# Seven experts' second product in seven block products instead of eight, rows added by accumulating DMAs, and a list schedule for the expert stage

## The chip, the cores and the metric

The kernel runs on one core of one Trainium2 chip. The metric is device time in microseconds (us) of one execution, as a median over runs. The profile was taken from one further execution. Engines are named PE (matrix products), PEld (PE's weight loads), DVE, ACT, POOL (element-wise engines) and SP, which here only issues transfers (DMAs).

## The reference

Attention for 4 batches of 8 heads (576 tokens, width 64) gives x, 2304 rows of 512. A gate gives each row a weight for each of 8 experts (softmax, then 8 rounds of normalising rows and columns). The output is the weighted sum of all experts over all rows:

```python
logits = x @ w_gate
P = np.exp(logits - logits.max())
for _ in range(8):
    P /= P.sum(1, keepdims=True) + 1e-09
    P /= P.sum(0, keepdims=True) + 1e-09
    P *= N / E
for e in range(E):                    # 8 experts: 512 -> 1024 -> 512
    h = np.maximum(x @ w1[e], 0.0)
    out += P[:, e:e + 1] * (h @ w2[e])
```

## The kernel before

Everything is float32 in and out. Matrix products run in float16: each operand is split into a high half and a low half (the remainder), and each product is the sum of three partial products, high by high, high by low and low by high. The splits are element-wise work: ACT writes the high half ("h" in names such as `w1h`), DVE or POOL writes the low half.

The program has two stages. The first holds attention, expert 0 and the gate; a list scheduler (`class Plan`) sets the order of its instructions. It gets each step with an assumed duration (`US`), a due time, its inputs and the buffers that it takes, and writes one fixed order for each engine. At its end the prepared block sums of x are stored (`x_sums`) and the weights of the first half expert are split.

The second stage holds experts 1 to 7. Each expert is cut into two halves of 512 hidden columns, which makes 14 **half experts** (`PH`). For each of these the rows are walked in five blocks (`BLK`): the rows form two halves of 1152, and a block takes 256 rows from each half, the last block 128 ("half block"). So a half expert is 4 full blocks and one half block, 4.5 blocks in all. A block has two products.

- First product, W1 by x: written as a product of 2 by 2 blocks that needs seven block products instead of eight (Winograd's form). These are `M1` to `M7` (`mm1`); each is 12 matmuls of w columns (w is 256, or 128 in a half block), whose left operands are blocks of W1 or sums of blocks (A11, A12, A22, S1 to S4) and whose right operands are blocks of x or sums of them, loaded again for each block (`ts`). The results land in four PSUM banks a to d, and DVE, ACT and POOL add them up: `m1`, `u2`, `u3`, `c12`, `c21` and `c22`. Then ACT and DVE write the relu of the four blocks as high and low halves into a tile `h` (`relu_hi`, `relu_lo`).
- Second product, h by W2 (`mm2`, steps `T0` to `T3`): for each of 4 tiles of 128 rows (2 in a half block) 12 matmuls of 512 columns. DVE multiplies the PSUM tile by the gate weight and adds it to the output accumulator in SBUF, `accA` or `accB` (`out_add`, L1165).

The order in the second stage is a table written by hand, `BLOCK_AT` with a `PERIOD` of 19.6: all steps of all blocks sorted by their place. The next half expert's weights are loaded and prepared meanwhile by a generator, `w_prep`, one step at fixed intervals (`SIDE_EVERY`). It takes the maximum of each weight tile (`absmax` on DVE, then across the partitions with POOL's `partition_all_reduce`, L221), scales to a power of two, splits seven blocks of W1 (low halves at L253) with four block sums on POOL in between (L1078 to L1089), and then four pieces of W2 without sums. The last lines of the sorting:

```python
    for n in sorted(range(len(plan)), key=lambda n: (plan[n][0], n)):
        plan[n][1]()
```

## Time and profile before

| what | value |
|---|---|
| median of 3 runs | 1782.56 us (1782.41 to 1786.26) |
| the profiled execution, its own time | 1782.06 us |
| its span, first to last instruction | 1780.2 us |
| PE busy | 1734.9 us, 97% of the span |
| DVE, ACT, POOL busy | 1107.1, 661.2, 506.9 us |

The span is what the rows below divide up; some 1.9 us of the execution's own time lie around it. Busy time is an average over both stages. PE's records overlap, since matmuls are pipelined, so that the time of one matmul is read from a run of many, not from its own duration.

### The profile page before, as it was taken

How to read it: one execution, taken by the hardware profiler on the slowest of the kernel's cores; microseconds unless marked ns; L12 is line 12 of the kernel's file. 1: busy time of each engine (PE TensorE's matmuls, PEld its weight loads, DVE VectorE, ACT ScalarE, POOL GpSimd, SP SyncE). 2: the span in 40 equal slices, each digit the busy share in tenths (PEclk: the TensorE clock that was granted, in tenths of full speed). 3: DMA queues.
4: the chain of work that ended last, by engine and by line, in shares of the span. 5: the costliest groups of instructions: out<-in, count | busy, mean ns of one | idle time of the engine just before them, and what ended most of it. 6: DMA issues, size and time to landing. Idle time of an engine off the chain costs nothing.

```text
span 1780.2 us, 32960 instructions
## 1 busy us (share of the span) xinstructions
PE 1734.9 (97%) x13860; PEld 1085.4 (61%) x13860; DVE 1107.1 (62%) x1849; ACT 661.2 (37%) x1157; POOL 506.9 (28%) x435
## 2 busy tenths in 40 slices
PE   5989999999999999999999999999999999999999
PEld 3455455554456566666666666666666666666665
DVE  7978757641895565656565656565756574656543
ACT  3568777775334332323222222222323232222221
POOL 3467788875332010201010202020202020202000
PEclk8999999999999999999999999999999999999999
DMA  5323122101023122222221222131313131213122
GB/s 203 114 93 98 42 66 95 42 17 39 24 95 115 54 82 81 74 83 88 68 90 66 88 67 106 49 107 48 107 48 107 48 107 52 103 48 107 51 89 87
DMA packets 47645, 140.18 MB, mean 79 GB/s; under 512 B 12436, under 2 KB 16904, under 8 KB 43400
## 3 DMA queue, kind: packets, MB, share of 16 engines
q1 hardware_dynamic: 47496, 138.08, 23.4%
q8 instruction: 108, 1.77, 0.4%
q14 instruction: 41, 0.34, 0.1%
HBM read 128.41 MB, written 9.64 MB: 78 GB/s over the span
## 4 chain that ended last, share of the span: by engine, by line
PE 86%; DVE 6%; DMA 3%; ACT 2%; issue 2%; POOL 1%; SPq 0%; POOLq 0%; ACTq 0%; DVEq 0%
PE m L1157 34%; PE m L1141 30%; PE g L718 5%; PE g L697 5%; PE s L415 3%; PE t L471 3%; PE av L507 3%; PE t L468 2%; DMA wraw<-in_w 1%; DVE mraw L416 1%; PE as L521 1%; DVE w1l L253 1%; DVE h L1182 1%; DMA s<-sd 1%; PE av L501 0%
## 5 line engine op out<-in xcount | busy, mean ns | idle before, releaser
L1157 PE MATMUL m<-w2h,h 128*128 128x512 f16 x2016 | 641.6, 380 | 0.0
L1157 PEld LDWEIGHTS <-h 128*128 128x128 f16 x3024 | 294.0, 98 | 303.4 <-issue 2.1
L1141 PEld LDWEIGHTS <-w1h 128*128 128x128 f16 x3920 | 369.4, 98 | 97.2 <-issue 7.0
L1157 PE MATMUL m<-w2l,h 128*128 128x512 f16 x1008 | 382.6, 380 | 0.0
L1141 PE MATMUL m<-ts,w1h 128*128 128x256 f16 (+1 forms) x2240 | 349.0, 262 | 1.0 <-DVE u L1173 1.0
L1173 POOL TENSOR_TENSOR c<-u,t 128x512 f32<-128x512 f32 (+1 forms) x70 | 81.8, 1169 | 826.2 <-DVE u L1173 734.2
L1178 ACT ACTIVATE h<-c 128x512 f16<-128x512 f32 (+1 forms) x210 | 117.3, 583 | 464.4 <-DVE c L1173 429.1
L1141 PE MATMUL m<-ts,w1l 128*128 128x256 f16 (+1 forms) x1120 | 284.6, 262 | 0.0
L1141 PE MATMUL m<-xx,w1h 128*128 128x256 f16 (+1 forms) x1680 | 261.9, 262 | 5.1 <-ACT m L1170 5.1
L1141 PE MATMUL m<-xx,w1l 128*128 128x256 f16 (+1 forms) x840 | 213.6, 262 | 0.0
L1182 DVE SCALAR_TENSOR_TENSOR h<-c,h 128x512 f16<-128x512 f32 (+1 forms) x210 | 144.4, 710 | 101.9 <-ACT h L1178 101.5
L1141 PEld LDWEIGHTS <-w1l 128*128 128x128 f16 x1960 | 191.7, 98 | 17.8
L1165 DVE SCALAR_TENSOR_TENSOR accA<-m,pp,accA 128x512 f32<-128x512 f32 x168 | 125.4, 746 | 76.6 <-PE m L1157 76.3
L486 POOL TENSOR_TENSOR eb<-e,eb 128x576 f16<-128x576 f32 x117 | 158.8, 1371 | 37.1 <-ACT eb L483 32.8
L416 DVE TENSOR_REDUCE mraw<-s 128x2 f32<-128x576 f32 x140 | 105.3, 752 | 63.9 <-PE s L415 62.7
L1165 DVE SCALAR_TENSOR_TENSOR accB<-m,pp,accB 128x512 f32<-128x512 f32 x84 | 63.0, 750 | 111.8 <-PE m L1157 111.8
L1170 ACT COPY t<-m 128x512 f32<-128x512 f32 (+1 forms) x70 | 37.9, 541 | 206.8 <-PE m L1141 206.8
L1173 DVE TENSOR_TENSOR c<-m,u 128x512 f32<-128x512 f32 (+1 forms) x140 | 88.8, 634 | 39.4 <-PE m L1141 39.4
L479 ACT ACTIVATE e<-t,ebias,pc 128x576 f32<-128x576 f32 x117 | 97.3, 832 | 34.2 <-PE t L471 30.1
L342 POOL TENSOR_TENSOR raw<-raw,trig 128x576 f32<-128x576 f32 x61 | 92.4, 1528 | 36.5 <-DMA raw<-in_qk 19.0
L415 PE MATMUL s<-Z 64*128 64x288 f16 (+1 forms) x936 | 83.5, 289 | 15.7 <-DVE mraw L416 7.3
L257 ACT ACTIVATE w1h<-wraw,s 128x512 f16<-128x512 f32 x98 | 66.9, 715 | 65.7 <-DVE s L246 54.9
(160 smaller groups left out, 2086.8 us busy)
## 6 DMA issues: line engine op xcount, KB each, us to landing
ts<-xd SPq DMA_DIRECT2D x110, 512.0 KB
wraw<-in_w SPq DMA_DIRECT2D x28, 1024.0 KB
raw<-in_qk SPq DMA_DIRECT2D x32, 576.0 KB
ts<-xd SPq DMA_DIRECT2D x28, 256.0 KB
vraw<-in_v SPq DMA_DIRECT2D x4, 1280.0 KB
rs<-si SPq DMA_DIRECT2D x64, 72.0 KB
wraw<-in_w SPq DMA_DIRECT2D x8, 512.0 KB
xd<-ts SPq DMA_DIRECT2D x8, 512.0 KB
```

The source lines that it names most:

```text
L342: engine[e].tensor_tensor(r[:, t, :], r[:, t, :], trig[:, n, :], op=ALU.mult)
L415: pe.matmul(po[j], zz[r, x, qc], zz[r, y, QH[kh]], start=n_ == 0, stop=n_ == 2)
L416: return lambda: dve.reduce_max(o, ps[:, :, 0:HS], axis=AX.X)
L479: act.activation(e32, ps[:, :, 0:HS], AF.Exp, bias=ebias, scale=sc[p][0])
L486: engine[e].tensor_tensor(E[g][:, 1], e32, E[g][:, 0], op=ALU.subtract)
L697: pe.matmul(pv, a[:, hf, c, fh, j * P : (j + 1) * P], x[:, c, :, n0 : n0 + w], start=c == 0 and n == 0, stop=c == KC - 1 and n == 2,)
L1141: pe.matmul(live[bk][:, f * w : (f + 1) * w], x[:, a, i, fs], y[:, i], start=first and f == 0 and n == 0, stop=n == 5, skip_group_check=True,)
L1157: pe.matmul(po, x, y[:, ch], start=n == 0, stop=n == 11)
L1165: dve.scalar_tensor_tensor(o, pt.pop((th, j)), pp[e, hf][:, tt : tt + 1], o, op0=ALU.mult, op1=ALU.add)
L1173: engine[e_].tensor_tensor(temp(n, tag), live[x], live[y], **add)
L1178: act.activation(t[:, 0 : 2 * w], live[src], AF.Relu)
L1182: dve.scalar_tensor_tensor(f(hq[n][:, 1]), live[src], 0.0, f(hq[n][:, 0]), op0=ALU.max, op1=ALU.subtract)
```

## The change

Second product. The second product of experts 1 to 7 takes Winograd's form too. Its left operands are the four blocks A11, A12, A21 and A22 of h and four sums S1 to S4 of them (A21 is needed only inside the sums), its right operands three blocks of W2 and four sums T1 to T4. The seven block products `N1` to `N7` (table `G2_MM`) are 12 matmuls of 256 columns each, into four PSUM banks of their own (`ps_n`; `ps_m` holds four for the first product). A half block has 6 matmuls in each.

Element-wise work. In a block, DVE now computes u2, u3, c22, c12, c21, the sums S1 to S4, five low halves (A11, A12, S2, S3, S4), and U2, U3, C22, C21, C12 of the second product: 19 operations. POOL writes two low halves (A22 and S1, `LOC`). ACT makes m1, the relus, the seven high halves and n1, and scales the four result blocks by the gate weight into a tile `ev` (`out`; 8 instructions of 256 columns). In the last half expert DVE adds the result into the accumulator itself, as before.

Adding of rows. An `ev` tile is added to the accumulator by a DMA that POOL issues with `accum_op=ALU.add` (`deliver`, two a block, 512 KB each); there are three `ev` buffers.

Weights. W2 is split in seven pieces with four block sums, as W1 is. The maximum across partitions is taken on DVE: a transpose of 32 by 32 blocks, six small maxima and two small copies (`turn`), in place of POOL's all-reduce.

Order. The list scheduler also orders the second stage (`experts`), with due times worked out from block lengths and the offsets `SH2`, `LAG`, `WSH`; the hand-written table and the side generator go. `H_BUFS`, the number of h tiles (seven are used in a block now, four before), goes from 10 to 9.

```diff
-H_BUFS = 10
+H_BUFS = 9
+LAG = 2.1
+WSH = 10.0
+SH2 = dict(m1=0.7, o21=3.7, u2=-1.5, o12=-1.5, S2=1.5, S1l=0.7, A11l=-3, A12h=0.7, o11=3.7, c21=-1.5, N1=-3, c12=0.7, C21=1.5, N5=1.5, N7=0.7, S1h=1.5)
...
+LOC = dict(A22="pool", A11="dve", A12="dve", S1="pool", S2="dve", S3="dve", S4="dve")
...
-PERIOD = 19.6
-BLOCK_AT = dict(
-    begin=-0.1, middle=0.5, ld0=6.6, ld1=15.7, M1=0.0, M6=1.3, M5=5.2, M2=6.5, M7=10.4, M3=11.7, M4=15.6,
...
-    def gmax(mx, n, tag):
-        g = small.tile([P, n], F32, tag=tag + "g", name="g")
-        pool.partition_all_reduce(g, mx, P, RMAX)
...
-        r, s, hl = yield from start(w2, 2, 4)
-        for i in range(5):
-            if i < 4:
-                hi(hl, s, i, r[:, i * 512 : (i + 1) * 512], False)
-            if i:
-                lo(hl, s, i - 1, r[:, (i - 1) * 512 : i * 512], False)
...
+        def turn(d=d):
+            t = small.tile([P, 32], F32, tag="wt", name="wt")
+            dve.transpose(t, d["g"].to_broadcast([P, 32]))
+            y = small.tile([P, 4], F32, tag="wy", name="wy")
+            for b in range(4):
+                dve.reduce_max(y[0:32, b : b + 1], t[32 * b : 32 * b + 32], axis=AX.X)
+            g = small.tile([P, 1], F32, tag="wg2", name="wg2")
+            dve.reduce_max(g[0:32], y[0:32], axis=AX.X)
+            dve.tensor_copy(g[32:64], g[0:32])
+            dve.tensor_copy(g[64:P], g[0:64])
+            d["g2"] = g
...
+        def split(i, a, deps=()):
+            put(f"wh{i}", "act", US["wh"], lambda: hi(i, a), ["ws"] + list(deps), uses=[raw])
+            put(f"wl{i}", "dve", US["wl"], lambda: lo(i, a), [f"wh{i}"], uses=[raw], lock=True)
+
+        def total(k, o, x, y, op, deps):
+            put(k, "pool", US["ptt"], lambda: pool.tensor_tensor(quad(o), quad(x), quad(y), op=op), deps, uses=[raw])
...
+            split(B11, "11")
+            split(B22, "22")
+            split(B21, "21")
+            total("w+1", "11", "12", "11", ALU.subtract, [f"wl{B11}", "wm1"])
+            total("w+3", "12", "12", "22", ALU.subtract, ["w+1"])
+            total("w+2", "22", "22", "11", ALU.subtract, ["w+3", f"wl{B22}"])
+            total("w+4", "21", "21", "22", ALU.subtract, ["w+2", f"wl{B21}"])
+            split(T1, "11", ["w+1"])
+            split(T2, "22", ["w+2"])
+            split(T3, "12", ["w+3"])
+            split(T4, "21", ["w+4"])
...
+        def mm(bank, first, lhs, rhs, step, width, pl):
+            if first:
+                live[bank] = pl.tile([P, 512], F32, tag="g", name="m")[:, 0:cols]
+            (ah, al), (bh, bl) = lhs, rhs
+            for f_ in range(cols // width):
+                n = 0
+                for i in range(2):
+                    for x, y in ((ah, bh), (ah, bl), (al, bh)):
+                        pe.matmul(
+                            live[bank][:, f_ * width : (f_ + 1) * width], step(x, i, f_), y[:, i],
+                            start=first and f_ == 0 and n == 0, stop=n == 5, skip_group_check=True,
+                        )
+                        n += 1
...
-        def mm2(th, j):
-            if j >= nt:
...
-                h = hq[("c11", "c12", "c21", "c22")[2 * (ch // 2) + th]]
-                hh, hl = h[:, 0, ch % 2, js], h[:, 1, ch % 2, js]
-                for x, y in ((hh, wh), (hh, wl), (hl, wh)):
-                    pe.matmul(po, x, y[:, ch], start=n == 0, stop=n == 11)
-                    n += 1
...
-        def out_add(th, j):
-            if j >= nt:
-                return
-            tt = th * NT2 + k * (WB // P) + j
-            o = accs(tt)
-            dve.scalar_tensor_tensor(o, pt.pop((th, j)), pp[e, hf][:, tt : tt + 1], o, op0=ALU.mult, op1=ALU.add)
...
+        def mm2(bk, first, a, b):
+            lhs = [hq[a][:, n] for n in range(2)]
+            rhs = [x[:, b].rearrange("p (c f) -> p c f", c=2) for x in ws[q][2]]
+            mm("n" + bk, first, lhs, rhs, lambda x, i, f_: x[:, i, f_ * P : (f_ + 1) * P], 256, ps_n)
...
+        def op_lo(eng, n, src):
+            h, l = (hq[n][:, i].rearrange("p c w -> p (c w)") for i in range(2))
+            engine[eng].tensor_tensor(l, live[src], h, **sub)
+
+        def plus_lo(n, src):
+            h, l = (hq[n][:, i].rearrange("p c w -> p (c w)") for i in range(2))
+            dve.scalar_tensor_tensor(l, live[src], 0.0, h, op0=ALU.max, op1=ALU.subtract)
+
+        def plus_combine(n, x, y, op1):
+            dve.scalar_tensor_tensor(live[n], live[x], 0.0, live[y], op0=ALU.max, op1=op1)
...
+        def out(th, dh, src):
+            for j in range(nt):
+                tt = th * NT2 + k * (WB // P) + j
+                x, s = live[src][:, j * 256 : (j + 1) * 256], pp[e, hf][:, tt : tt + 1]
+                d = slice(dh * 256, dh * 256 + 256)
+                if final:
+                    o = accs(tt)[:, d]
+                    dve.scalar_tensor_tensor(o, x, s, o, op0=ALU.mult, op1=ALU.add)
+                else:
+                    if th not in ev:
+                        ev[th] = evp.tile([P, 2, DM], F32, tag="ev", bufs=3, name="ev")
+                    act.activation(ev[th][:, j, d], x, AF.Copy, scale=s)
+
+        def deliver(th):
+            t0_ = k * (WB // P)
+            if final:
+                for j in range(nt):
+                    store(th * NT2 + t0_ + j)
+            else:
+                a = accparts[0][:, th, t0_ : t0_ + nt] if t0_ < ACC_A else accparts[1][:, th, t0_ - ACC_A : t0_ - ACC_A + nt]
+                pool.dma_start(out=a, in_=ev[th][:, 0:nt], accum_op=ALU.add)
...
+        put("A22h", "act", rl, tm(3) + 1.3, lambda: op_hi("A22", "c22", AF.Copy), ["r22"], [("h", "A22")], [("c22", 0)])
+        put(
+            "A22l", LOC["A22"], on[LOC["A22"]], tm(3) + 1.9, lambda: op_lo(LOC["A22"], "A22", "c22"), ["A22h"], [],
+            [("h", "A22"), ("c22", 0)], lock=True)
...
+        put("c12", "dve", pa, tm(5), lambda: plus("c12", "c", "u2"), ["M3", "u2"], [("c12", 0)], [("m", "c"), ("u2", 0)])
+        put(
+            "S1", "dve", on["dve"], tm(5) + 0.7, lambda: plus_combine("c22", "c12", "c22", ALU.add), ["c12", "A22l"], [],
+            [("c12", 0), ("c22", 0)], lock=True)
+        put(
+            "S3", "dve", on["dve"], tm(5) + 2.0, lambda: plus_combine("c12", "c12", "r11", ALU.subtract), ["S1", "r11"], [],
+            [("c12", 0), ("r11", 0)], lock=True)
+        put(
+            "S2", "dve", on["dve"], tm(5) + 1.4, lambda: combine("dve", "r11", "c22", "r11", sub), ["S3", "A11l"], [],
+            [("c22", 0), ("r11", 0)], lock=True)
...
+    G2_MM = dict(
+        N1=("a", True, B11, "A11"), N6=("b", True, T2, "S2"), N5=("c", True, T1, "S1"), N2=("a", False, B21, "A12"),
+        N7=("d", True, T3, "S3"), N3=("c", False, B22, "S4"), N4=("d", False, T4, "A22"),
+    )
...
+    def experts():
+        plan = Plan(dict(
+            m=4, n=4, m1=1, u2=1, u3=1, c22=1, r11=1, c12=1, c21=1, n1=1, U2=1, U3=1, C21=1, ev=3, h=H_BUFS, ts=3, stg=1,
+            w1=2, w2=2,
+        ))
```

Three places in the order of the instructions. On PE, in the second stage, the boundary of a first-product piece and a second-product piece before the change (`w1h` and `w1l` are W1's halves, `w2h` and `w2l` those of W2, `xx` is x, `m` a PSUM tile):

```order
L1141 MATMUL m<-xx,w1l 128x256
L1157 LDWEIGHTS h
L1157 MATMUL m<-w2h,h 128x512
L1157 LDWEIGHTS h
L1157 MATMUL m<-w2l,h 128x512
```

The same boundary in the change:

```order
L1163 MATMUL m_16435<-xx_94,w1l_14843 128x256
L1163 LDWEIGHTS h_16357
L1163 MATMUL m_16362<-w2h_15470,h_16357 128x256
L1163 LDWEIGHTS h_16357
L1163 MATMUL m_16362<-w2l_15471,h_16357 128x256
```

What moved: the second product's matmuls have 256 columns and a weight load each, as those of the first product have had all along.

On DVE, the end of a full block in the second stage before the change (L1173 are the sums, L1182 the low halves of h, L1165 the adding to the accumulator):

```order
L1173 TENSOR_TENSOR u_12431<-m,u_12354 128x512 [waits DVE_49,PE_49]
L1173 TENSOR_TENSOR c_12448<-m,u_12354 128x512 [waits PE_49]
L1182 SCALAR_TENSOR_TENSOR h<-c_12448,h 128x512 [waits Activation_49]
L1182 SCALAR_TENSOR_TENSOR h<-c_12433,h 128x512 [waits Activation_49]
L1165 SCALAR_TENSOR_TENSOR accA<-m,pp,accA 128x512 [waits PE_49]
L1173 TENSOR_TENSOR c_12484<-m,u_12354 128x512 [waits PE_49]
L1182 SCALAR_TENSOR_TENSOR h<-c_12484,h 128x512 [waits Activation_49]
L1165 SCALAR_TENSOR_TENSOR accA<-m,pp,accA 128x512 [waits PE_49]
```

The same end of a block in the change (c with L1193 is c21, C is C21 of the second product of the block before, L1212 the low half of A12, L1215 S1 and S3, L1199 S2, L245 a low half of the next weights, L1344 C12, L1208 low halves):

```order
L1193 TENSOR_TENSOR c_15083<-m,u_14918 128x512 [waits DVE_49,PE_49]
L1193 TENSOR_TENSOR C_15099<-m,U_14958 128x512 [waits PE_49]
L1212 SCALAR_TENSOR_TENSOR h<-c_15083,h 128x512 [waits Activation_49]
L1215 SCALAR_TENSOR_TENSOR c_14976<-c_15044,c_14976 128x512 [waits Pool_49]
L1215 SCALAR_TENSOR_TENSOR c_15044<-c_15044,r_15011 128x512 [waits DVE_49]
L1199 TENSOR_TENSOR r_15011<-c_14976,r_15011 128x512 [waits DVE_49]
L245 SCALAR_TENSOR_TENSOR w1l<-wraw,s,w1h 128x512
L1344 TENSOR_TENSOR U_14958<-m,U_14958 128x512 [waits PE_49]
L1193 TENSOR_TENSOR u_15173<-m,m_15119 128x512 [waits PE_49,Activation_49]
L1208 TENSOR_TENSOR h<-r_15011,h 128x512 [waits Activation_49]
L1208 TENSOR_TENSOR h<-c_15044,h 128x512
```

What moved: the adding to the accumulator is gone from DVE, and between c21 and the low halves stand the sums S1, S3 and S2, of which S1 waits for POOL and the others for the one before.

On POOL, a stretch of the second stage before the change (L1173 is c22, L221 the all-reduce for a maximum, `wraw` the block sums of W1):

```order
L1078 TENSOR_TENSOR wraw<-wraw 128x2x256 [waits DMAHW4_49,DVE_49]
L1081 TENSOR_TENSOR wraw<-wraw 128x2x256 [waits Pool_49]
L1085 TENSOR_TENSOR wraw<-wraw 128x2x256 [waits DVE_49,Activation_49,Pool_49]
L1089 TENSOR_TENSOR wraw<-wraw 128x2x256 [waits DVE_49,Activation_49,Pool_49]
L1173 TENSOR_TENSOR c_12238<-u_12236,t_12190 128x512 [waits DVE_49,Activation_49]
L221 ISA
L221 ISA g<-wmx 128x2 [waits DVE_49]
```

The corresponding stretch in the change (L1208 are the low halves of A22 and S1, L1237 the accumulating DMAs, L1113 block sums of weights):

```order
L1208 TENSOR_TENSOR h<-c_12173,h 128x512 [waits PE_49,Activation_49,Pool_49]
L1208 TENSOR_TENSOR h<-c_12173,h 128x512 [waits DVE_49,PE_49,Activation_49]
L1237 DMA accA<-ev 128x1024 [waits DMASW6_49,Activation_49]
L1237 DMA accA<-ev 128x1024 [waits DMASW7_49,Activation_49]
L1113 TENSOR_TENSOR wraw<-wraw 128x2x256 [waits DMAHW1_49,DVE_49]
L1113 TENSOR_TENSOR wraw<-wraw 128x2x256 [waits Pool_49]
L1113 TENSOR_TENSOR wraw<-wraw 128x2x256 [waits DVE_49,Pool_49]
L1208 TENSOR_TENSOR h<-c_12464,h 128x512 [waits PE_49,Activation_49]
L1113 TENSOR_TENSOR wraw<-wraw 128x2x256 [waits DVE_49,Pool_49]
```

What moved: two accumulating DMAs and two low halves a block stand on POOL in place of c22 and the all-reduce, each DMA waiting for ACT's scaled rows and for an earlier DMA of its lane (DMASW), and W2 brings four more block sums for each half expert.

## Rows read from the trace of the kernel before

**Rows 1.** The page: busy time, share of the span and instructions of each engine.

```profile
PE 1734.9 (97%) x13860; PEld 1085.4 (61%) x13860; DVE 1107.1 (62%) x1849; ACT 661.2 (37%) x1157; POOL 506.9 (28%) x435
```

**Rows 2.** Busy time of the engines by stretch, granted clock, DMA share.

```profile
core 0: us, PE busy (x) PEld busy (x) DVE busy (x) ACT busy (x) POOL busy (x), PEclk, DMA share, GB/s
...
440.00:536.00 96.00, 95.11 (x540) 49.62 (x539) 82.42 (x165) 33.06 (x62) 36.50 (x30) 1.00 0.17 62
...
1240.00:1328.00 88.00, 88.00 (x637) 58.70 (x636) 54.60 (x83) 23.33 (x41) 13.11 (x11) 1.00 0.25 79
```

**Rows 3.** The chain that ended last, in order of time: start, us, what.

```profile
535.50 11.79 PE m L1141 x108
...
1154.76 2.59 PE m L1157 x12
1157.35 5.24 PE m L1141 x48
...
1240.18 2.62 PE m L1141 x24
...
1328.17 2.62 PE m L1141 x24
...
1768.25 7.78 PE m L1157 x36
```

**Rows 4.** PE's waits: us in total, times, longest us.

```profile
PE m L1141 <- ACT m L1170: 5.1, 4, 2.3
```

**Rows 5.** DVE's groups by shape in the second stage (count, busy us, mean ns).

```profile
L1182 DVE SCALAR_TENSOR_TENSOR h<-c,h 128x512 f16<-128x512 f32 x168 | 127.7, 782 | 88.4 <-ACT h L1178 87.9
...
L253 DVE SCALAR_TENSOR_TENSOR w1l<-wraw,s,w1h 128x512 f16<-128x512 f32 x91 | 83.5, 929 | 1.6 <-ACT w1h L257 0.9
L1173 DVE TENSOR_TENSOR c<-m,u 128x512 f32<-128x512 f32 x112 | 76.9, 687 | 36.0 <-PE m L1141 36.0
...
L253 DVE SCALAR_TENSOR_TENSOR w2l<-wraw,s,w2h 128x512 f16<-128x512 f32 x52 | 37.8, 745 | 2.1 <-ACT w2h L257 2.1
...
L1173 DVE TENSOR_TENSOR c<-m,u 128x256 f32<-128x256 f32 x28 | 11.9, 425 | 3.4 <-PE m L1141 3.4
```

**Rows 6.** DVE in order of time: start, us, tiles, count.

```profile
1252.06 1.29 DVE L1182 SCALAR_TENSOR_TENSOR h<-c,h 128x512 f16<-128x512 f32 x2 [0.70 <-ACT h L1178]
...
1260.45 2.33 DVE L250 TENSOR_REDUCE wmx<-wraw 128x1 f32<-128x1024 f32 x2
...
1266.91 0.14 DVE L1054 TENSOR_REDUCE wg<-g 128x1 f32<-128x2 f32 x1
1267.09 0.15 DVE L240 TENSOR_SCALAR e<-wg 128x1 int32<-128x1 int32 x1
...
1281.41 1.40 DVE L253 SCALAR_TENSOR_TENSOR w1l<-wraw,s,w1h 128x512 f16<-128x512 f32 x2
```

**Rows 7.** POOL and DVE side by side in order of time.

```profile
1270.08 1.26 POOL L1173 TENSOR_TENSOR c<-u,t 128x512 f32<-128x512 f32 x1 [6.78 <-ACT w1h L257]
1270.16 1.73 DVE L1182 SCALAR_TENSOR_TENSOR h<-c,h 128x512 f16<-128x512 f32 x1 [0.99 <-ACT h L1178]
1271.31 1.70 POOL L1078 TENSOR_TENSOR wraw<-wraw 128x512 f32<-128x512 f32 x1
```

**Rows 8.** Groups of ACT and POOL by shape in the second stage.

```profile
L1178 ACT ACTIVATE h<-c 128x512 f16<-128x512 f32 x168 | 101.3, 626 | 372.9 <-DVE c L1173 337.6 <-POOL c L1173 35.3
...
L1173 POOL TENSOR_TENSOR c<-u,t 128x512 f32<-128x512 f32 x56 | 71.7, 1280 | 619.3 <-DVE u L1173 527.2 <-DVE h L1182 35.0 <-issue 22.2
...
L1081 POOL TENSOR_TENSOR wraw<-wraw 128x512 f32<-128x512 f32 x13 | 20.8, 1603 | 1.0
...
L1178 ACT ACTIVATE h<-c 128x256 f16<-128x256 f32 x42 | 16.0, 412 | 91.6 <-DVE c L1173 91.6
```

**Rows 9.** A 1 MB load of weights, issued by SP, and its first reader.

```profile
1282.84 0.33 SPq L1038 DMA_DIRECT2D wraw<-in_w  x1
...
1287.68 1.22 DVE L250 TENSOR_REDUCE wmx<-wraw 128x1 f32<-128x1024 f32 x1 [1.15 <-DMA wraw<-in_w]
```

More of the change, by code (lines that the diff above doesn't have):

```diff
@@ L108, in run @@
         held, ready = {}, {e: set() for e in LATENCY}
[L109 removed]
+        free = {e: self.busy.get(e, 0.0) for e in LATENCY}
         begun, on, events, order = [False] * len(ops), {}, [], []
@@ L1109, in block_ops, with put, load, half_max @@
-    def block_ops(c):
+        d = {}
+        def put(k, eng, us, fn, deps, **kw):
+            nonlocal at
+            at += gap
+            plan.add(f"{k}.{n}.{q}", (eng, us), at + (SH2.get(k[0:2], 0.0) if q else 0.0), fn, [x if "." in x else f"{x}.{n}.{q}" for x in deps], **kw)
+        def load(d=d, w=w):
+            d["r"] = stg.tile([P, 2048], F32, tag="raw", name="wraw")
+            sp.dma_start(out=d["r"], in_=w[e, hf])
+        def half_max(i, d=d):
+            if i == 0:
+                d["mx"] = small.tile([P, 2], F32, tag="wmx", name="wmx")
+            absmax(d["mx"][:, i : i + 1], d["r"][:, i * 1024 : i * 1024 + 1024])
@@ new lines, in both @@
+        def both(d=d):
+            d["g"] = small.tile([P, 1], F32, tag="wg1", name="wg1")
+            dve.reduce_max(d["g"], d["mx"], axis=AX.X)
+        def turn(d=d):
[9 more added lines that the diff above has]
+            d["g2"] = g
@@ new lines, in scale @@
+        def scale(d=d, n=n):
+            d["s"], winv[e, hf, n] = pow2_of(d["g2"], 1, 2 if n == 1 else 13, f"w{n}")
+            d["hl"] = [wS[q % 2].tile([P, 7, 512], F16, tag=f"w{n}{x}", name=f"w{n}{x}") for x in "hl"]
+            ws.setdefault(q, {})[n] = d["hl"]
+        raw = ("stg", (q, n))
+        if q == 0:
+            put("wd", "sp", 7.0, load, last, allocs=[raw])
+        else:
+            put("wd", "sp", 9.5, load, last, allocs=[raw])
+        put("wm0", "dve", US["w"], lambda f=half_max: f(0), ["wd"], uses=[raw])
@@ new lines, in block_ops, with ahead @@
+        lin = lambda a, b: a + b * f
+        wl = (lambda n, i: [f"wl{i}.{n}.{q}"]) if q else (lambda n, i: [])
+        pa, cp, rl = lin(0.07, 0.535), lin(0.05, 0.43), lin(0.1, 0.43)
+        on = dict(pool=lin(0.06, 1.18), dve=lin(0.07, 0.535))
+        if c + 1 < len(PH) * len(BLK):
+            k1 = (k + 1) % len(BLK)
+            for i in range(2):
+                def ahead(i=i):
+                    xt_sb[c + 1, i] = sums_load(k1, i)
+                plan.add(f"ld{i}.{c + 1}", ("sp", 5.5), t0 + gap * (1 + 3 * i), ahead, allocs=[("ts", (c + 1, i))])
@@ new lines, in block_ops @@
+        put("c21", "dve", pa, tm(6), lambda: plus("c21", "d", "u2"), ["M4", "u2"], [("c21", 0)], [("m", "d"), ("u2", 0)])
+        put("A12h", "act", rl, tm(6) + 0.7, lambda: op_hi("A12", "c21", AF.Relu), ["c21"], [("h", "A12")], [("c21", 0)])
+        if LOC["A12"] == "dve":
+            put(
+                "A12l", "dve", on["dve"], tm(6) + 1.4, lambda: plus_lo("A12", "c21"), ["A12h"], [], [("h", "A12"), ("c21", 0)],
+                lock=True)
+        put(
+            "S4", "dve", on["dve"], tm(6) + 2.0, lambda: plus_combine("c21", "c21", "r11", ALU.subtract), ["S2", "A12l"], [],
+            [("c21", 0), ("r11", 0)], lock=True)
@@ new lines, in block_ops @@
+        for n, src, at in (("S2", "r11", tm(5) + 2.1), ("S3", "c12", tm(5) + 2.7), ("S1", "c22", tm(5) + 3.3), ("S4", "c21", tm(6) + 2.7)):
+            put(n + "h", "act", rl, at, lambda n=n, src=src: op_hi(n, src, AF.Copy), [n], [("h", n)], [(src, 0)])
+            e_ = LOC[n]
+            put(
+                n + "l", e_, on[e_], at + 0.6, lambda n=n, src=src, e_=e_: op_lo(e_, n, src), [n + "h"], [],
+                [("h", n), (src, 0)], lock=True,
+            )
+        k2 = BLK[(k + 1) % len(BLK)][1]
@@ L1283, in late_ops @@
     def late_ops():
-        plan.add("rel", ("none", 0.0), 0, rel, [f"l{j}.{p}" for j in range(2) for p in range(NPAIR)] + ["le.3"])
+        plan.add("rel.0", ("none", 0.0), 0, rel, [f"l{j}.{p}" for j in range(2) for p in range(NPAIR)] + ["le.3"])
         d = lambda us, *r: ("dve", us, [], r)
@@ L1312, in attention_moe @@
     plan.run()
-    run(prep_q)
-    for x in (hB, hA, wA):
+    for x in (ps_h, ps_1, ps_g, hB, hA, wA):
         x.release()
+    ps_m, ps_n = (mkpool(x, 4, space=PSUM) for x in ("ps_m", "ps_n"))
     wS[1] = mkpool("wS1")
     hS = mkpool("hS")
-    nb = len(PH) * len(BLK)
-    plan = [x for c in range(nb) for x in block_ops(c)]
-    plan += [(t * SIDE_EVERY, side) for t in range(int(PERIOD * nb / SIDE_EVERY))]
-    for n in sorted(range(len(plan)), key=lambda n: (plan[n][0], n)):
-        plan[n][1]()
-    for x in (ps_h, ps_1, ps_g, tmp, strm, stg, wS[0], accq, accp[0], hS, wS[1], big, small, const, dram):
+    evp = mkpool("evp")
+    Plan.last = experts()
+    for x in (ps_n, ps_m, tmp, strm, stg, wS[0], accq, accp[0], evp, hS, wS[1], big, small, const, dram):
         x.release()
```

337 lines of the change are left out of this document (172 added, 165 removed).

## The prediction

> **What bounds the kernel now.** I read the page first: PE is busy for 97% of the span, DVE for 62% [rows 1]. Such shares mix two stages, so the stretches came next: in 1240 to 1328 us PE is busy for all of 88.0 us at full clock (1.00, 2.4 GHz), DVE for 54.6, ACT for 23.3, POOL for 13.1 [rows 2]. The chain in order of time then gives the structure. The first matmul of experts 1 to 7 starts at 535.5 us, the pattern repeats after 88.0 us (1240.18 and 1328.17), which is one half expert, and the chain is PE from end to end [rows 3]. 14 times 88.0 is 1232; 1780.2 less 535.5 less 1232 leaves 12.7 us for the tail. PE's waits confirm it: the longest entry of the second stage is 5.1 us, in four waits [rows 4]. So PE sets the time of that stage, and whatever takes columns off PE is worth its full price until another engine fills up.
>
> **PE.** A run of 48 matmuls of 256 columns takes 5.24 us, 109 ns each; 12 of 512 columns take 2.59 us, 216 ns each [rows 3]. The second product of a full block now costs 48 times 216 ns, 10.4 us, and in the change 84 times 109 ns, 9.2 us: 1.2 us less. In a half block 24 of 512 columns (5.2 us) become 42 of 256 (4.6 us): 0.6 less. A half expert gains 4 times 1.23 and 0.6, 5.5 us, and becomes 82.5 us; 14 of them gain 77 us. The first product, of the same matmul shape with as many weight loads, already runs at 109 ns in runs of 48, so the doubled weight loads need no price. 82.5 us is the floor.
>
> **DVE** is what must be weighed against it. What it starts without waiting costs less than its duration: two low halves of 0.69 us take 1.29 us, so the second starts 0.60 after the first; two weight low halves take 1.40, 0.65 apart; two maxima 2.33; small operations start 0.18 apart [rows 6]. By the order of the instructions one half expert in the change has 76 operations of 512 columns (45.6 us at 0.60), 19 of 256 (6.5 us at 0.34, from 0.425 [rows 5] less the same overlap), 14 weight low halves (9.1), 4 maxima (4.7) and 26 small ones (4.7): 70.6 us. 18 stand right behind the operation that they wait for, like S1, S3, S2 in the order shown, and pay 0.69 instead of 0.60: 1.6 more. That is 72.2 us of 82.5; if every operation waited for the end of the one before, 81.0 us would be the upper bound.
>
> Two things come on top. **First, collisions with POOL.** A DVE operation with both inputs in SBUF that starts beside a POOL operation takes 1.73 us instead of 0.69, ending 0.55 us after POOL's ends; the next POOL operation then takes 1.70 [rows 7]. Before, such operations pay on average 0.09 us (low halves of h, 782 against 690 ns), 0.18 (W1's, 929 against 745) or nothing (W2's, 745) [rows 5], while POOL is busy for 13.1 of 88.0 us, 15% [rows 2]. In the change POOL has 8 operations at 1.28 us, two at half that and 8 weight sums at up to 1.60 [rows 8]: 24 us of 82.5, 29%, beside 54 exposed DVE operations (the sums and low halves of h in SBUF, and 14 weight low halves). Bounds: nothing each, or 0.36, twice the worst group. I take 0.12: about the mixed price of before (0.10), since POOL is there twice as often but the new order was laid out to keep such pairs apart and part of that should survive. 54 times 0.12 is 6.5 us. **Second, waits for ACT.** In the order shown the low half of A12 stands two places behind c21; ACT's high half of 0.63 us [rows 8] comes between, so DVE stands for some 0.5 us in each block, 2.2 us in a half expert.
>
> DVE's sum is 72.2 + 6.5 + 2.2 = 80.9 us against PE's 82.5. Two engines at 98% and 100%, each with a fixed order and few buffers, do not mesh perfectly; I add 1.8 us to the longer one (between 0 and the 5.5 that would eat the gain) and take **84.3 us** for a half expert. The last has no weights to prepare and adds its rows on DVE, 36 operations of 256 columns, some 13 us in place of the 19 for weights: 82.8.
>
> **The rest.** ACT: 11 operations of about 0.6 us and 8 of 0.41 in a full block [rows 8], with 14 weight high halves in each half expert some 12 us of 18.3: hidden, and if it were not, it would show as DVE waiting for ACT. DVE's new maxima (18 of the 26 small operations) are in the sum; the POOL all-reduce that they replace was hidden. Taking the adding to the accumulator off DVE is in the sum as well, four operations less a block. The accumulating DMAs have no row: for the issue on POOL the nearest are SP's 0.33 us [rows 9] and, above, POOL's longest element-wise row, 1.60; nine in a half expert are 3 to 14 us on an engine that is 29% busy, hidden either way, with the low halves behind them on POOL late by that much at most. For the landing the nearest row is a load of 1 MB, 4.84 us from issue to first reader [rows 9]. 512 KB read twice and written once take between half of that and, at 1.5 times the bytes, 7.3 us. Two of three buffers fill in a block; each is held some 7 us before its DMA is issued, so that landing may take 14 us before ACT has to wait. Costed at nothing. Before the second stage W2's three more splits and four sums come to DVE and POOL, which are busy for 82.4 and 36.5 of 96 us while PE has 95.1 [rows 2]: 2 us on DVE into 13.6 us of room; I put 1.0 us for it and for the change of PSUM pools. The tail now has a chain through S4, its halves, N3 and C12 in place of one low half and three tiles (7.78 us [rows 3]): 2.0 us more.
>
> **Sum.** 535.5 + 1.0 + 13 times 84.3 + 82.8 + 12.7 + 2.0 = 1729.9 us of span; 1.9 around it as before, and 0.5 by which the median of before lies above its profiled execution: **1732 us**, 2.8% less.
>
> **A rule against it.** [Rows 7] show DVE standing until POOL has finished. The Trainium skill, page "SBUF — State Buffer", section "SBUF: two separate sides", says that VectorE and GpSimd share a port pair as an exclusive lock, taken for a whole instruction against VectorE operations with two SBUF inputs, and that the loser blocks fully. The trace agrees, 1.73 against 0.69 us. By the rule with starts at random the sum is that of the second rival.
>
> **Rivals.** *PE alone bounds* (22%): collisions stay near zero, as for W2's low halves now [rows 5], and nothing is added to 82.5: 1709 us. *Collisions at random* (18%): a DVE start meets POOL in 29% of cases and waits for half of 1.28 us, 0.19 each, 10.3 us; DVE then needs 84.7 and with the same 1.8 us a half expert takes 86.5: 1761. Speaking for it: W1's low halves pay 0.18 now. *DVE falls behind, slower* (10%): the same place, S1 to S4 and the low halves; from 0.25 us a collision DVE needs the 88.0 of before, and at 0.33, nearly the bound, 92.2: 1835 us. Against it: such a price was only seen in single rows. *Accumulating DMAs too slow* (6%): three buffers, two a block, give a block of two thirds of (7 us + landing); past 22 us of landing it is slower than the 19.56 of now, at 24 us 20.7 a block, some 1850. Against it: 4.84 us for twice the bytes. *No gain on PE* (4%), if a long stretch with a weight load for every 109 ns cannot keep the pace: at 124 ns a half expert is back at 88 and the time at 1782 to 1790. For it: PE never ran more than some hundred such matmuls in a row; against it: those went at 109.
>
> **How the numbers follow.** 40% stand on the forecast, whose own range is 1715 to 1752. The range reaches from the PE floor with a little less tail, 1706, over the random collisions to 1785; above lie most of the slow cases. A measurement of this kernel tells about 0.2% from no change (its runs lie 0.2% apart). Faster: the forecast, PE alone, random collisions, 80%; same 4%; slower 16%.
>
> **What would show it.** Right: half experts repeat at 83 to 86 us, runs of 12 matmuls of 256 columns at 1.31 us in both products, DVE busy over 90%, PE's waits naming DVE, a few tenths each. Wrong: PE's waits naming ACT behind a DMA (buffers), POOL's operations near 1.7 us and DVE's low halves above 0.9 on average (collisions), or gaps in PE in the weight-laden blocks alone, whose places in the order were set by assumed durations.

## The result and the profile after

The changed kernel takes **1744.4 us** (median of 4 runs, 1743.1 to 1747.2) against 1784.1 us before (4 runs, 1782.4 to 1786.3): a ratio of 0.9779, 95% interval 0.9761 to 0.9797. The forecast was 1732 us. The gain is 40 us where 50 were forecast (1782.6 to 1732).

The page after, as [rows 1] before, and its largest row of adding transfers (KB each, median us from issue to landing; accB's of the same size show 5.8):

```profile
PE 1667.3 (96%) x16128; PEld 1305.9 (75%) x16128; DVE 1492.4 (86%) x2653; ACT 1050.0 (60%) x2017; POOL 775.7 (45%) x665
...
accA<-ev POOLq DMA_DIRECT2D x78, 512.0 KB, 5.5
```

DVE has gone from 62% to 86%; PE is still the busiest. A half expert of the second stage by the view of stretches, against [rows 2]; the next one shows 85.39:

```profile
core 0: us, PE busy (x) PEld busy (x) DVE busy (x) ACT busy (x) POOL busy (x), PEclk, DMA share, GB/s
...
1133.02:1218.42 85.40, 83.20 (x798) 74.47 (x798) 79.40 (x139) 52.00 (x105) 32.30 (x28) 1.00 0.55 136
```

A half expert repeats at 85.40 us (88.0 before, 84.3 forecast) and PE stands in it for 2.2 us at full clock. The largest entry among PE's waits in the whole span (us in total, times, longest):

```profile
PE m L1163 <- DVE U L1193: 30.1, 26, 2.1
```

26 waits are two in each of the 13 half experts that prepare weights, both for the sums U2 and U3 of the second product; in the stretch shown they are 1.74 and 0.47 us. The chain, against [rows 3], shows what is late ahead of the longer one:

```profile
1133.02 21.89 PE m L1163 x198
...
1204.02 0.69 DVE C L1193
...
1205.91 1.57 DVE h L1212
1207.48 2.27 DVE wmx L242 x2
...
1215.13 0.49 DVE ec L942
...
1215.65 1.33 DVE pp L944
1216.98 0.61 DVE U L1193
...
1218.42 21.89 PE m L1163 x198
```

From 1204.02 to 1218.42 the chain lies on DVE: low halves, W2's maxima and its turned maximum, then ec and pp (the factor of the half expert's rows, one column and 18), then U2 and U3. Three durations there are odd. DVE and POOL side by side in order of time, one half expert earlier; the last two rows are ec and pp of the first half expert, where POOL is idle:

```profile
1120.44 1.65 DVE L1212 SCALAR_TENSOR_TENSOR h<-c,h 128x512 f16<-128x512 f32 x1
...
1129.65 0.56 DVE L942 TENSOR_TENSOR ec<-inv 128x1 f32<-128x1 f32 x1
1130.25 1.33 DVE L944 TENSOR_SCALAR pp<-prob,ec 128x18 f32<-128x18 f32 x1
...
1119.94 1.60 POOL L1208 TENSOR_TENSOR h<-c,h 128x512 f16<-128x512 f32 x1 [8.11 <-DVE h L1208]
...
1128.93 2.61 POOL L1113 TENSOR_TENSOR wraw<-wraw 128x512 f32<-128x512 f32 x2 [6.58 <-DVE w2l L245]
...
538.96 0.14 DVE L942 TENSOR_TENSOR ec<-inv 128x1 f32<-128x1 f32 x1
539.13 0.24 DVE L944 TENSOR_SCALAR pp<-prob,ec 128x18 f32<-128x18 f32 x1
```

It is the collision of [rows 7] again: POOL's two weight sums run from 1128.93 to 1131.54, and pp ends at 1131.58. Two operations worth 0.38 us take 1.89 in each of the 13 later half experts. A12's low half pays 0.97 us beside a low half on POOL in the same way. DVE's groups in four half experts (count, busy us, mean ns), as in [rows 5]:

```profile
L245 DVE SCALAR_TENSOR_TENSOR w1l<-wraw,s,w1h 128x512 f16<-128x512 f32 x28 | 31.2, 1127 | 0.0
L245 DVE SCALAR_TENSOR_TENSOR w2l<-wraw,s,w2h 128x512 f16<-128x512 f32 x28 | 24.5, 875 | 0.0
L1215 DVE SCALAR_TENSOR_TENSOR c<-c,r 128x512 f32<-128x512 f32 x32 | 24.2, 758 | 0.3
...
L1212 DVE SCALAR_TENSOR_TENSOR h<-c,h 128x512 f16<-128x512 f32 x16 | 14.8, 924 | 0.0
...
L944 DVE TENSOR_SCALAR pp<-prob,ec 128x18 f32<-128x18 f32 x4 | 5.3, 1328 | 0.1
```

W1's low halves went from 929 to 1127 ns, W2's from 745 to 875.

**Theory:** PE's floor and DVE's sum were about right, and what lies above the floor is made at fixed places on DVE, by collisions with POOL and by small operations ahead of U2 and U3. **Rivals:** DVE's plain load; PE itself, which cannot keep 109 ns with a weight load for each matmul; the adding transfers.

### The profile page after: what moved, and what is told of

Its sections match the earlier page's. It is cut to its first block, busy times and chain, and to the rows that moved or that the text cites. A ratio compares the mean times of both kernels' runs of the same rounds, so it can differ in the third digit from the quotient of the medians.

```text
span 1742.8 us, 39818 instructions
## 1 busy us (share of the span) xinstructions
PE 1667.3 (96%) x16128; PEld 1305.9 (75%) x16128; DVE 1492.4 (86%) x2653; ACT 1050.0 (60%) x2017; POOL 775.7 (45%) x665
## 4 chain that ended last, share of the span: by engine, by line
PE 70%; DVE 23%; issue 2%; DMA 2%; ACT 2%; SPq 0%; POOL 0%; DVEq 0%; ACTq 0%; POOLq 0%
PE m L1163 48%; PE g L710 5%; PE g L689 4%; DVE wmx L242 4%; PE s L407 3%; PE av L499 3%; PE t L463 3%; DVE h L1212 2%; DVE U L1193 2%; DVE h L1208 2%; PE t L460 2%; DVE c L1215 1%; DVE c L1193 1%; DVE wy L1056 1%; DVE mraw L408 1%
## 5 line engine op out<-in xcount | busy, mean ns | idle before, releaser
L1163 PE MATMUL m<-w2h,h 128*128 128x256 f16 x3528 | 626.6, 273 | 31.6 <-DVE U L1193 30.1
L1163 PEld LDWEIGHTS <-h 128*128 128x128 f16 x5292 | 514.3, 98 | 97.8 <-issue 34.4
L1163 PE MATMUL m<-w2l,h 128*128 128x256 f16 x1764 | 480.9, 273 | 0.0
L1208 POOL TENSOR_TENSOR h<-c,h 128x512 f16<-128x512 f32 (+1 forms) x140 | 176.1, 1258 | 548.1 <-ACT h L1204 372.5
L1113 POOL TENSOR_TENSOR wraw<-wraw 128x512 f32<-128x512 f32 x112 | 159.8, 1427 | 176.2 <-DVE w2l L245 130.8
L1204 ACT ACTIVATE h<-c 128x512 f16<-128x512 f32 (+1 forms) x350 | 199.4, 581 | 55.2 <-DVE c L1215 29.3
L1228 ACT ACTIVATE ev<-U,pp 128x256 f32<-128x256 f32 x234 | 106.9, 499 | 93.0 <-DVE U L1336 63.2
L1193 DVE TENSOR_TENSOR c<-m,u 128x512 f32<-128x512 f32 (+1 forms) x210 | 132.7, 632 | 17.2 <-PE m L1163 10.2
L249 ACT ACTIVATE w2h<-wraw,s 128x512 f16<-128x512 f32 x98 | 67.6, 716 | 76.9 <-DVE s L238 68.9
L245 DVE SCALAR_TENSOR_TENSOR w1l<-wraw,s,w1h 128x512 f16<-128x512 f32 x98 | 106.3, 1097 | 0.0
L1215 DVE SCALAR_TENSOR_TENSOR c<-c,r 128x512 f32<-128x512 f32 (+1 forms) x140 | 102.5, 732 | 1.2
```

What stands on the lines that cost most here:

```text
L245: dve.scalar_tensor_tensor(lo, x, s, hi, op0=ALU.mult, op1=ALU.subtract)
L1113: put(k, "pool", US["ptt"], lambda: pool.tensor_tensor(quad(o), quad(x), quad(y), op=op), deps, uses=[raw])
L1163: pe.matmul(live[bank][:, f_ * width : (f_ + 1) * width], step(x, i, f_), y[:, i], start=first and f_ == 0 and n == 0, stop=n == 5, skip_g ...
L1193: dve.tensor_tensor(o, live[x], live[y], **add)
L1204: act.activation(t[:, 0:cols], live[src], func)
L1208: engine[eng].tensor_tensor(l, live[src], h, **sub)
```

## The experiments

All kernels are the changed one with the edit shown; "repeat" is the time from one half expert to the next, read from the trace. Differences are taken from the repeats: the first stage is the same in all these kernels, yet in their eleven traces the first matmul of experts 1 to 7 starts between 538.9 and 545.1 us, and that is part of every time. So turn_late saves 12 times 0.61, 7.3 us, in its repeats, but its time is only 3.8 us shorter (its start is 5.0 us later).

| kernel | repeat, us | time, us |
|---|---|---|
| changed kernel | 85.40 | 1744.4 |
| ec and pp moved (pp_early) | 84.32 | 1730.9 |
| low half moved (swap_low) | 84.43 | 1732.5 |
| turned maximum of W1 moved (turn_late) | 84.79 | 1740.6 |
| all three moves (both) | 82.75 | 1711.4 |
| weights reused (reuse_w) | 82.74 | 1713.4 |
| no weight sums (no_sums) | 84.07 | 1731.6 |
| no adding transfers (no_deliver) | 85.39 | 1745.0 |
| rows added by DVE (add_dve) | 99.33 | 1924.9 |
| maximum by POOL's all-reduce (allreduce) | 92.4 (mean) | 1837.8 |
| ec and pp kept apart by the schedule (pp_lock) | 86.54 | 1756.7 |

**ec and pp moved.** The schedule is made as before; pp's place is left empty.

```diff
-            plan.add(f"pp.{q}", ("dve", 0.5), a + 6, lambda e=e, hf=hf: expert_p(e, hf), ...
+            plan.add(f"pp.{q}", ("dve", 0.5), a + 6, lambda e=e, hf=hf, q=q: None if q else expert_p(e, hf), ...
...
             ws.setdefault(q, {})[n] = d["hl"]
+            if q and n == 2:
+                expert_p(e, hf)
```

> The two small operations that form the factor of each half expert (ec and pp, 0.56 and 1.33 us on DVE while POOL forms weight sums, 0.14 and 0.24 in the one half expert where POOL is idle) are issued nine DVE places earlier, right behind the scale of W2, where POOL is idle; same engine, same work, nothing else moved. Collision theory: they take 0.38 us together, U2 and U3 come 1.5 us earlier, PE's gap of 1.74 us in each half expert shrinks to about 0.25, half experts repeat at 83.9 us instead of 85.40, and the time is 1744.4 - 13 x 1.5 = 1725 us. Rival, that DVE's plain work in front of U2 and U3 (maxima, turned maximum, scale) makes the gap: the work is the same, so 85.4 us and 1744.

Measured: 1730.87 us (1729.58 to 1732.91, 4 runs), a ratio to before of 0.9709 (0.9691 to 0.9727). The chain:

```profile
1128.39 0.61 ACT w2h L249
1129.01 0.79 ACT ev L1230 x2
...
1130.59 19.07 PE m L1165 x172
...
1214.90 19.06 PE m L1165 x172
```

84.32 us. The same work on the same engine, clear of POOL, is worth 1.08 us in each half expert: the collision, not the load. It isn't the 1.5 us expected, since ACT's work is next at that place (the first two rows; a high half on ACT and its low half on DVE follow before PE).

**The low half moved**, and all else as in the change. The order that the schedule gives is edited by hand before it is issued, on DVE only (`nm`: the names in that order; `behind(x, y)` puts x behind y; q is the half expert, 1 to 13):

```diff
+            i = nm.index(f"wm0.2.{q}")
+            behind([x for x in nm[:i] if x[0:5] == "A12l."][-1], nm[i])
```

> One place of DVE's order in each half expert is changed: the low half of A12 ahead of W2's two maxima, which waits for a low half on POOL (1.65 us instead of 0.69), stands behind the first maximum; everything else as in the changed kernel, ec and pp too. Collision theory: the maximum reads SBUF once and is not held up, the low half then finds POOL idle, so the chain ahead of the 1.74 us gap is 0.9 us shorter: 84.5 us a half expert, 1733 us. Rival: the maximum itself is held up beside POOL, or the low half is late for someone else, and the repeat stays at 85.4 us, 1744.

Measured: 1732.5 us (one run). The order in time and the chain:

```profile
1114.57 1.60 POOL L1218 TENSOR_TENSOR h<-c,h 128x512 f16<-128x512 f32 x1 [8.11 <-DVE h L1218]
...
1115.07 1.21 DVE L252 TENSOR_REDUCE wmx<-wraw 128x1 f32<-128x1024 f32 x1
1116.20 0.68 DVE L1222 SCALAR_TENSOR_TENSOR h<-c,h 128x512 f16<-128x512 f32 x1
```

```profile
1126.71 21.89 PE m L1173 x198
...
1211.14 21.89 PE m L1173 x198
```

As expected. The maximum, which reads one tile of SBUF, runs beside POOL at its usual 1.21 us; the low half behind it takes 0.68 instead of 1.65.

**The turned maximum of W1 moved**, and **all three moves**. The diff is the last move; the third kernel has all.

```diff
+            if q < 2:
+                continue
+            i = nm.index(f"wt.1.{q}")
+            behind(nm[i], [x for x in nm[i:] if x[0:3] == "U3."][0])
```

> Of the three moves only the last: the turned maximum of W1 (1.55 us on DVE) stands behind U2 and U3 instead of ahead of them; ec, pp and A12's low half where the change has them. Theory, fixed places on DVE, each gap with its own cause: the gap of 0.47 us closes, with the 0.1 or so that PE needs to restart, the one of 1.74 us stays; 84.9 us a half expert, 1737 us. Rival, that one gap only moves time into the other: 85.4 us, 1744.

> Three moves on DVE together: ec and pp behind W2's scale, A12's low half behind the first maximum of W2, and the turned maximum of W1 (1.55 us) behind U2 and U3 instead of ahead of them. Theory, that fixed places on DVE make all that lies above PE's floor of 82.74 us: both gaps close; 83.2 us a half expert, 1744.4 - 13 x 2.2 = 1716 us. Rival, from the trace with ec and pp moved alone (84.32 us, PE now waits behind ACT's row copies at the place of the old gap): ACT takes over there and only the second gap closes, 83.8 us, 1724.

Measured: 1740.6 us (one run) for the move alone; 1711.36 us (1710.62 to 1712.99, 4 runs) for all three, a ratio to before of 0.9613 (0.9596 to 0.963). The chain of the first:

```profile
1132.66 70.36 PE m L1175 x642
1217.45 70.36 PE m L1175 x642
```

A stretch of the second, which its chain crosses on PE alone (columns as above):

```profile
618.00:1640.00 1022.00, 1022.00 (x9856) 918.52 (x9854) 949.13 (x1713) 642.34 (x1300) 395.89 (x350) 1.00 0.58 141
```

The short gap closes alone (84.79). With all three PE's waits show no entry in 1022 us: 9856 matmuls there, 798 in a half expert, give 82.75 us. That is below the 83.2 expected; ACT, which stood behind the gap in the first experiment, no longer shows. At 1711.4 us this kernel is faster than the change as well as than the kernel before.

**Weights reused.** `reuse` hands on the tiles of two half experts before.

```diff
+            if q > 1:
+                fn = reuse if k == "ws" else lambda: None
             plan.add(f"{k}.{n}.{q}", (eng, us), ...
```

> Weights of half experts 2 to 13 are left out: no load, maximum, split or sum for them, the tiles of the first two half experts are used again. DVE loses about 24 us in a half expert, POOL its sums. If DVE alone holds PE up, PE runs at its floor: 82.5 us a half expert, 1744.4 - 12 x 2.9 = 1710 us. Rival, that part of the 2.9 us above the floor is PE's own (a weight load for every 109 ns, over hundreds of matmuls) or ACT's and the transfers': 84 us or more, 1727.

Measured: 1713.4 us (one run). The chain is PE alone from 1100 to 1290 us. pp, which comes once in a half expert, in order of time:

```profile
1112.44 0.23 DVE L944 TENSOR_SCALAR pp<-prob,ec 128x18 f32<-128x18 f32 x1
...
1195.18 0.24 DVE L944 TENSOR_SCALAR pp<-prob,ec 128x18 f32<-128x18 f32 x1
```

82.74 us, without a wait of PE: the floor, forecast at 82.5. So PE itself, with a weight load for every matmul, has no part in what lies above it. This run alone doesn't clear ACT and the transfers, since ACT's weight halves and the weight loads are gone too; the kernel with all three moves does, where they are all in place.

**No weight sums.**

```diff
-            put(k, "pool", US["ptt"], lambda: pool.tensor_tensor(quad(o), quad(x), quad(y), op=op), deps, uses=[raw])
+            put(k, "pool", US["ptt"], lambda: q or pool.tensor_tensor(quad(o), quad(x), quad(y), op=op), deps, uses=[raw])
```

> The eight weight sums of each half expert from the second on are left out on POOL, so that products S and T take plain quarters; every other instruction stays in its place. Collision theory: ec and pp take 0.4 us, W1's low halves 0.75 instead of 1.13, W2's 0.75 instead of 0.88; the gap ahead of U2 and U3 shrinks to 0.3 us, 83.8 us a half expert, 1723. Rival (plain DVE work, or collisions with POOL's low halves of h alone): ec and pp fast, but the gap stays above 1 us, 85 us, 1739.

Measured: 1731.6 us (one run), 84.07 us a half expert. DVE's groups:

```profile
L245 DVE SCALAR_TENSOR_TENSOR w1l<-wraw,s,w1h 128x512 f16<-128x512 f32 x28 | 31.3, 1129 | 1.3 <-ACT w1h L249 1.3
...
L245 DVE SCALAR_TENSOR_TENSOR w2l<-wraw,s,w2h 128x512 f16<-128x512 f32 x32 | 23.8, 743 | 0.0
...
L944 DVE TENSOR_SCALAR pp<-prob,ec 128x18 f32<-128x18 f32 x4 | 0.9, 236 | 0.1
```

W2's low halves and pp are free without the sums, pp at its old place: the second test of that collision. W1's are not, against what I expected: with the sums gone they still take 1129 ns, and what POOL then has are its low halves of h.

**No adding transfers**, and **rows added by DVE**.

```diff
-                pool.dma_start(out=a, in_=ev[th][:, 0:nt], accum_op=ALU.add)
+                pass
```

```diff
-        oe, ou = ("dve", 2 * lin(0.1, 0.28)) if final else ("act", lin(0.36, 0.42))
+        oe, ou = ("dve", 2 * lin(0.1, 0.28))
...
-                if final:
+                if True:
                     o = accs(tt)[:, d]
                     dve.scalar_tensor_tensor(o, x, s, o, op0=ALU.mult, op1=ALU.add)
...
-            if final:
-                for j in range(nt):
+            if final or True:
+                for j in range(nt if final else 0):
```

> The adding transfers of half experts 0 to 12 are left out, so their rows are not added; ACT still scales them into the three buffers. If the transfers (0.88 us of POOL for each issue, 5.5 us to landing) are hidden as the prediction has it: 85.4 us a half expert within 0.3, 1740 to 1746 us. Rival, that they hold up ACT by buffers or POOL's low halves by the issues: 84.5 us or less, 1733.

> The adding transfers alone are undone: DVE adds the scaled rows to the accumulator itself, 36 operations of 256 columns in each half expert at 0.34 to 0.48 us (the last half expert's take 0.48 in a row), and ACT's 36 row copies and POOL's 9 issues go; the list schedule is made anew with these operations. If DVE is the engine next to the bound: 79.4 + 12 to 17 us gives 92 to 96 us a half expert, 1830 to 1880 us. Rival, that DVE has room and the transfers bring little: 86 to 87 us, 1760.

Measured: 1745.0 us without the transfers, 1924.9 with the rows added on DVE (one run each). The chain of the first:

```profile
1132.92 21.89 PE m L1163 x198
...
1218.31 21.89 PE m L1163 x198
```

85.39 us: the transfers cost nothing. The chain of the second:

```profile
1164.18 25.07 PE m L1163 x228
...
1263.51 25.06 PE m L1163 x228
```

99.33 us, 14 more than the change, and more than the 92 to 96 expected. Pairs of adds start 0.40 us apart (0.79 for two in its chain), so 36 are 14.2 on top of 79.4: 93.6. That sum holds: in this repeat DVE is busy for 94.05 us. In the other 5.3 it waits, in the new order that the list schedule made; in that order PE also stops once for 4.7 us, and behind it its granted clock is 0.52 in 1215.3 to 1218.3 us. What each makes of the 5.3 stays open. With the rows added by DVE in this order the change would be slower than the kernel before; no other way of adding them was tried.

**Maximum by POOL's all-reduce**, in the slot of the eight DVE operations.

```diff
         def turn(d=d):
-            t = small.tile([P, 32], F32, tag="wt", name="wt")
-            dve.transpose(t, d["g"].to_broadcast([P, 32]))
...
+            g = small.tile([P, 1], F32, tag="wg2", name="wg2")
+            pool.partition_all_reduce(g, d["g"], P, bass_isa.ReduceOp.max)
             d["g2"] = g
```

> The maximum over partitions goes back to POOL's all-reduce (0.37 us in the kernel before) at the same place in the order; eight small DVE operations go, twice in a half expert. Collision theory: ahead of the gap DVE wins 1.55 us of chain and pays about 0.6 for waiting on POOL, so the 1.74 us gap falls to about 0.8 while ec and pp stay at 1.9 us, and the second gap of 0.47 us closes; 84.0 us a half expert, 1726 us. Rival, that the DVE-only chain is the better one because POOL is held up by its low halves, sums and transfers when the all-reduce is due: DVE waits 2 us or more for POOL, the gap grows, 86 us or more, 1752.

Measured: 1837.76 us (1837.49 to 1839.66, 4 runs), a ratio to before of 1.0313 (1.0297 to 1.033). DVE and POOL in order of time:

```profile
1171.70 0.15 DVE L1049 TENSOR_REDUCE wg<-wmx 128x1 f32<-128x2 f32 x1
1176.22 0.15 DVE L232 TENSOR_SCALAR e<-wg 128x1 int32<-128x1 int32 x1 [4.37 <-POOL wg L1053]
...
1168.81 0.87 POOL L1230 DMA_DIRECT2D accA<-ev  x1
1175.81 0.38 POOL L1053 PARTITION_ALL_REDUCE wg<-wg  x1 [6.14 <-issue]
1183.09 2.75 POOL L1106 TENSOR_TENSOR wraw<-wraw 128x512 f32<-128x512 f32 x2 [6.91 <-DVE U L1329]
```

The rival's range holds (86 us or more), its reason doesn't. The maximum is ready at 1171.85, POOL has been idle since 1169.68, and the all-reduce starts at 1175.81; the sums behind it start 6.9 us after its end, though their low half on DVE was done at 1178.94. At the start of both times POOL's queue has a pair of instructions, at 1169.6 and at 1176.1 us. Those ahead of the 26 all-reduces (count, ns least, median and most, first and last start):

```profile
L1053 POOLq MODIFY_POOL_CONFIG  x52: 1/160/319, 556.0 to 1723.0; - x52
```

DVE's eight operations (a transpose, five maxima and two copies) take 1.55 us. The starts of pp lie 91.5 to 94.0 us apart, 92.4 on average of the last 12, so this part of the change, forecast as a small cost on DVE, is worth 7.0 us a half expert at this place of the order.

About half of the 7.0 is PE's clock. Of the repeat from 1096.37 to 1188.44 us PE stands for 5.8 us, 3.6 more than in the changed kernel, and behind its two long stops (2.5 and 2.6 us) its granted clock falls to 0.50, which is 1.2 GHz (stretches, columns as above):

```profile
1178.50:1181.50 3.00, 3.00 (x18) 2.29 (x17) 2.76 (x7) 2.28 (x6) 0.00 (x0) 0.50 0.03 5
1188.50:1191.50 3.00, 3.00 (x15) 2.15 (x16) 2.78 (x4) 2.69 (x6) 2.31 (x2) 0.50 0.48 89
```

Products of 256 columns start 0.21 us apart there instead of 0.109; the two stretches at half clock, some 3.4 us each, cost about as much as one of them, 3.4 us. 82.74 + 5.8 + 3.4 is 91.9 of the 92.07 in that repeat. The order wasn't made for the all-reduce; whether another would hide it here, as the kernel before does, wasn't tried.

**ec and pp kept apart by the schedule.**

```diff
-            plan.add(f"pp.{q}", ("dve", 0.5), a + 6, ..., [f"ws.1.{q}", f"ws.2.{q}"] if q else [])
+            plan.add(f"pp.{q}", ("dve", 0.35), a + 6, ..., [f"ws.1.{q}", f"ws.2.{q}"] if q else [], lock=True)
```

> The list schedule is told about ec and pp what it is told about the low halves: that they must not stand beside an operation on POOL, and that they take 0.35 us; nothing else is edited, but the order that it then makes differs from the changed kernel's in some 600 places of DVE. If its rule of keeping apart works on the chip for them: 0.14 and 0.24 us each, and the repeat falls by about 1 us as with the move by hand, 84.3 us, 1730 us. Rival: the assumed durations drift from the real ones, so that in the new order other operations meet POOL at a place that matters, 85 us or more, 1740.

Measured: 1756.7 us (one run), slower than the change. The chain and DVE's groups:

```profile
1144.53 17.02 PE m L1163 x154
...
1231.07 17.02 PE m L1163 x154
```

```profile
L245 DVE SCALAR_TENSOR_TENSOR w2l<-wraw,s,w2h 128x512 f16<-128x512 f32 x28 | 28.5, 1040 | 0.0
...
L1215 DVE SCALAR_TENSOR_TENSOR c<-c,c 128x512 f32<-128x512 f32 x16 | 15.2, 953 | 0.4
...
L944 DVE TENSOR_SCALAR pp<-prob,ec 128x18 f32<-128x18 f32 x4 | 0.9, 236 | 0.1
```

The rival's number holds: pp is fast, but in the new order W2's low halves (875 to 1040 ns) and S1 (688 to 953) pay more, W1's low halves less (1127 to 836), and 86.54 us is 1.1 worse. Which of some 600 changed places makes the 1.1 us wasn't taken apart. A rule kept in assumed time doesn't keep operations apart on the chip: A12's low half and W1's carry the same rule in the changed kernel and meet POOL there.

## Why the prediction was right, and where it was off

**The bound and PE's floor: right.** PE sets the stage, matmuls of 256 columns hold 109 ns with a weight load each, and the floor is 82.74 us (forecast 82.5). The rival without gain on PE falls; the one in which PE alone bounds describes the kernel with all three moves.

**DVE's sum: about right, its parts not.** DVE is busy for 79.4 us of a half expert (forecast 78.7 of work, 80.9 with waits). The forecast time rests on PE's floor and the mesh, so this agreement doesn't carry it. The price of a collision, 0.12 us on 54 exposed operations, comes out by the groups: W1's low halves 7 times 0.39 over a clean 0.74, W2's 7 times 0.135, A12's 4 times 0.24, S1 to S4 and the half block some 1.2 in all, 5.8 us or 0.11 each. The wait for ACT behind c21 was put at 2.2 us; DVE's waits show none there, 0.4 us in a half expert at the low half of A11, and 1.1 at the sum u2 (the copy of M1 behind ACT's row copies).

**The step that failed is the mesh of the two engines, 1.8 us on the longer one, together with pricing ec and pp as small operations 0.18 apart.** The 1.8 stood on no row, so that it came within 0.9 us is luck. Measured are 85.40 less 82.74, 2.66 us (2.2 of it are PE's waits, the other 0.46 lie within its busy time, 83.20 us against 82.74). Moves of single operations take it apart: ec and pp alone 1.08, A12's low half alone 0.97, W1's turned maximum alone 0.61, together 2.66; all three moves together give 2.65. The first two are collisions, the third is plain small work ahead of U2 and U3. That the repeat is the forecast 84.3 with ec and pp clear of POOL is chance: what is left then is the other two places. Of the prediction's signs of being wrong, gaps in PE in the weight-laden blocks alone did come. I left ec and pp out of the 54 because they are small, but the price of a collision is POOL's operation, not DVE's own. And I spread collisions evenly as load, where the order repeats exactly: the same operations meet in every half expert, and only those ahead of a sum that PE waits for cost time (W1's low halves pay most and cost PE nothing that a gap shows). [Rows 7] fit the rule that the Trainium skill gives in "SBUF — State Buffer", "SBUF: two separate sides", a lock held for a whole instruction against DVE operations with two SBUF inputs. The trace agrees: 1.65 us against 0.68 for A12's low half. pp, which has one tensor and a scalar for each partition as inputs, is held as well, 1.33 us against 0.24. The same section of the Trainium skill, under "Who interferes with whom", also counts tensor_scalar, which pp is, among the operations that can take the pair in a two-port mode; no run here shows whether that is what holds pp.

**Start and ends.** The span of 1742.8 us exceeds 1729.9 by 12.9. Twelve repeats make 12 times 1.10, 13.2 us, and one of them takes 2.0 more (87.4 us): its longer stop is 2.1 us, and behind it the granted clock is 0.50, 1.2 GHz, from 962 to 965 us. The first matmul of experts 1 to 7 comes at 538.87 us instead of the 536.5 of the sum, +2.4; PE's waits for the gate's probabilities are 1.5 us longer in that stretch (2.2 against 0.7), but a start differs by up to 6.2 us between traces with the same first stage, so the 2.4 can't be put down to the change. The first and last half experts with the tail are 4.7 us shorter than put.

**Costed at nothing: held.** Issue on POOL takes 0.86 to 0.88 us, at most 1.22 (bounds 0.33 and 1.60), landing of 512 KB 5.5 to 5.8 us in the median (2.4 to 7.3), at most 9.8, under the 14 that the prediction put as harmless, and the repeat is the same without the transfers. The rivals of slow transfers and of DVE falling behind fall; DVE does fall behind when it has to add the rows itself.

## What to carry to other kernels

When two engines run at over 90% of a stage in a fixed order, find the one or two sums that the bounding engine waits for and read what stands ahead of them operation by operation; here ec and pp, two small operations that meet the other engine there, cost PE 1.08 us, while W1's seven low halves pay 2.7 us in collisions behind which no gap shows. Price such a meeting by the other engine's operation, and count every small operation. And once a list schedule has made an order, mend single places by hand from the trace: telling the schedule one more rule made a whole new order here, with new meetings. Before a long stop is priced by its length, look at the granted clock behind it.
